# Two attention blocks run twice on one core: quartered loads, a redrawn plan, and a first chunk of x that is turned by TensorE

## The chip, the core and the metric

One core of a Trainium2 chip runs the whole program. The metric is the device time of one execution in microseconds, lower being better. Several executions are made of each kernel and the median is compared; beside them stands one execution that was recorded by the hardware profiler, from which all durations here are taken.

## The reference

x has 2048 rows of 1024 bf16 values. Four blocks follow each other, A, B, A, B, each adding its result to x:

```
x = x + A(layernorm(x), A_wqkv, A_w_phi, A_wo)
x = x + B(layernorm(x), B_wqkv, B_wo)
x = x + A(...)      # the same weights as the first time
x = x + B(...)

A: q,k,v = x @ wqkv, 32 heads of 32 columns
   phi(t) = [softmax(t @ w_phi), softmax(-t @ w_phi)]
   out = phi(q) @ (phi(k)^T v) / (phi(q) . sum phi(k)),  then @ wo
B: ordinary softmax attention over 2048 keys, 32 heads of 32 columns, then @ wo
```

Block A is linear in the rows: its cost is projections. Block B needs 32 x 2048 x 2048 exponentials each time.

## The kernel before, in words

x is kept transposed in SBUF the whole time, in `xT`: 128 partitions, 8 groups of 128 columns of x (`PO`), 2048 rows. The rows are worked in four chunks of 512 (`NC`). Everything else lives in one big SBUF tile, `arena`, and one PSUM tile of eight banks, which the program divides itself.

**A planner sets the order.** The kernel function doesn't issue instructions; it records operations with `op(engine, duration, function, dependencies, buffers, priority)`. `Sched.run` (line 152) then plays a list schedule with those assumed durations: at each moment each engine takes, among the operations that are ready and whose buffers can be had (quotas in `QUOTA`, line 302), the one with the lowest priority number. The sequence in which operations start in that play is the sequence in which instructions are issued to the engines, and `_alloc` (line 77) fixes the buffers' addresses in the same play. So a change of one assumed duration can change the order of all that comes later, on every engine, and the addresses. Loads go through `dma` (line 474), on SyncE's queue ("SP") or ScalarE's queue ("AQ"); the planner assumes 0.55 us for an issue and 2 us plus a time by size for the landing.

**The first layer's start.** `load_x` (line 510) loads x with transposing DMAs on SyncE's queue: eight for the first chunk of 512 rows (one for each of the 8 column groups), eight for the second, eight for the last two together. Four small loads bring `w_phi` into `phi` (line 1215). `fold_phi` (line 599) multiplies the key part of A's weights, Wk, with the block-diagonal `phi`: two loads of 1 MB on ScalarE's queue bring Wk as it lies (line 603), 64 TensorE transposes in eight groups of eight turn it (line 612), each group is copied out of PSUM, in turn by ScalarE (line 620) and VectorE (line 617), 64 matmuls multiply (line 639), and ScalarE and VectorE in turn write the results (lines 646 and 649) into two slabs that hold 512 columns each. The slabs are also stored to DRAM (line 653) for the second time block A runs. `layernorm` (line 526) of a chunk: squares on ScalarE (line 538, in two halves here, n=2), 8 matmuls with a matrix of ones for the mean and 8 for the mean square (through `mmgroup`, line 480), mean and its square on ScalarE (559, 561), variance on VectorE (562), logarithm and exponential on ScalarE (564, 566), then for each quarter a subtraction and a multiplication on VectorE (572, 576). `a_keys` (line 668) then takes, for each 128 rows and 512 columns, 8 matmuls with the Wk slab and 8 with the Wv slab, two exponentials on ScalarE (688), a sum, a reciprocal and a product on VectorE (692, 695, 701). Matmuls of the plain kind all show as line 480, those that run on four column strips as line 484.

**The rest.** `a_queries`, `a_out`, and the projections of block B follow; then `attention` (line 1066) for 32 heads: scores in PSUM (line 1104), one exponential over three banks on ScalarE (line 1113), the product with V and with ones (line 1145), and its copy by VectorE (line 1161). Part of the exponentials is done on VectorE instead (`exp_dve`, lines 1047 to 1061). While ScalarE works through them, TensorE fills in other projections, among them the keys of the next block A. When TensorE has too little to do, the planner puts in matmuls that change nothing (line 1377). The second layer repeats all this, with its own constants.

**Loads of weights.** `slab` (line 582) loads 1024 rows by n columns of a weight as 128 partitions x 8 groups x n, with one DMA: 1 MB at n=512, 256 KB at n=128. It returns the load four times, one for each pair of the 8 groups, so that matmuls can depend on it pair by pair; before, the four are the same DMA. For the second layer, the normalized chunks 0 to 2 of block A come back from DRAM with one load of 1 MB each (line 1262).

Of the kernel before, what the change touches and what calls it, by code (L numbers as in the profile page):

```python
# [3 lines left out]

# [41 lines left out]
SWITCH = 0.1  # L46
AGAIN = 0.2
RING = 0.5
LOOK = 8


class Sched:
# [97 lines left out]
            b.at = None  # L150

    def run(self):
        engines = list(LAT)
        ready = {e: [] for e in engines}
        busy = {e: 0.0 for e in engines}
# [25 lines left out]
        while left:  # L181
# [109 lines left out]
NUMS = 2  # L291
# [7 lines left out]
EVAC = 20.0  # L299
QA = (40.0, 7.0)  # L300
KVG = 0.14
QUOTA = {"pk": 3, "pv": 2, "kv": 1, "ln": 2, "mm": 4, "cmp": 2, "bc": 4, "num": NUMS, "wt": 4, "fil": 2,
         "e": 6, "vp": 6, "e1": 4, "vp1": 4, "E": 6, "q2": 3, "kt": 3, "w2": 6, "w2o": 3, "oT": 27, "T": 4, "den": 2,
         "lnt": 6, "lnw": 2, "lnw1": 1, "eq": 16, "ns": 4, "cw": 6, "hl": 6, "oc": 2, "slab": 7, "slabk": 3, "fin": 4,
         "rs": 8, "pkf": 1, "cden": 2, "part": 8, "w2r": 1,
# [22 lines left out]
def dve_us(n):  # L328
    return n / 960 + 0.15
# [6 lines left out]
def kernel(  # L336
# [137 lines left out]
    def dma(prio, fn, deps=(), bufs=(), q="SP", kb=256, issue=0.55):  # L474
        return op(q, issue, fn, deps, bufs, prio, lat=2.0 + kb / 200.0)
# [32 lines left out]
    xdone = [None] * NC  # L508

    def load_x():  # L510
        for lo, hi, prio, us, kb in ((0, 1, -24.0, 1.3, 128), (1, 2, -9.0, 1.3, 400), (2, NC, -8.0, 2.0, 800)):
            last = []
            for po in range(PO):
                last.append(dma(
                    prio, lambda lo=lo, hi=hi, po=po: nc.sync.dma_start_transpose(
                        out=xT[:, po, lo * C512:hi * C512], in_=A_x[0, lo * C512:hi * C512, po * P:(po + 1) * P]),
                    issue=us, kb=kb))
            for c in range(lo, hi):
                xdone[c] = last
# [61 lines left out]

    def slab(cls, prio, src, n, deps=(), q="SP"):
        b, v = sb(cls, PO, n)
        o = dma(prio, lambda: (nc.sync if q == "SP" else nc.scalar).dma_start(out=v(), in_=src),
                deps, [b], q=q, kb=2 * n)
        return b, v, [o] * 4


    def slab_turned(cls, prio, src, n):
# [9 lines left out]
    def fold_phi(col, wd_v, prio, use_pe):  # L599
        w_t = []  # L600
        if use_pe:
# [4 lines left out]
            for g in range(G):  # L606
                tb, tv = ps("wt", ANY)

                def tr(g=g, tv=tv):
                    o = tv().bitcast(BF16)  # L610
                    for po in range(PO):
                        nc.tensor.transpose(
                            out=o[:, po * P:(po + 1) * P], in_=nv()[:, po, g * P:(g + 1) * P], identity=ident[:])
                t1 = op("PE", 8 * 0.11, tr, [ld[g // 4]], [tb, nb], prio, mode="n")
                wb, wv_ = sb("wT", D)
                if g % 2:
                    t2 = op("DVE", dve_us(1024), lambda tv=tv, wv_=wv_: nc.vector.tensor_copy(
                        out=wv_(), in_=tv().bitcast(BF16)), [t1], [tb, wb], prio)
                else:
                    t2 = op("ACT", act_us(1024), lambda tv=tv, wv_=wv_: nc.scalar.copy(  # L620
                        out=wv_(), in_=tv().bitcast(BF16)), [t1], [tb, wb], prio)
                w_t.append((wb, wv_, t2))
# [609 lines left out]
    for layer in range(2):  # L1232
# [14 lines left out]
            wv_s = [wv_slab(base + fc * 0.5, fc) for fc in range(2)]  # L1247
            chunks = range(NC - 1, NC)
        for c in chunks:
            xnA[c] = layernorm(c, base + 10 * c - 9 if base + c else -16.0, ANY, n=4 if layer else 2)  # L1250
            a_keys(c, base + 10 * c, wk_s, wv_s, kv, ANY)
        state = a_state(kv, base + 32)

# [3 lines left out]
        else:  # L1257
            wq_s = [slab("slab", second - 15 + fc, wdq_v[:, :, fc * C512:(fc + 1) * C512], C512, [store["q"][fc]])
                    for fc in range(2)]
            for c in range(NC - 1):  # L1260
                x_b, x_v = sb("xn", PO, C512)
                xnA[c] = (x_b, x_v, [dma(second - 20 + 20 * c, lambda c=c, x_v=x_v: nc.sync.dma_start(
                    out=x_v(), in_=xd_v[:, c, :, :]), [xnA[c]], [x_b], kb=1024)] * 4)
        wo_s = [slab_turned("slab", second - 6 + fc, A_o[:, :, fc * C512:(fc + 1) * C512], C512) for fc in range(2)]
        bv_s = [slab("slab", second - 4 + 134 * fc, B_w[:, :, 2 * D + fc * C512:2 * D + (fc + 1) * C512], C512)
                for fc in range(2)]
# [146 lines left out]
```

## Time and profile before

| what | value |
|---|---|
| median of 3 executions | 2373.57 us (2373.34 to 2375.6) |
| the profiled execution's own time | 2381.73 us |
| its span, first to last instruction | 2379.9 us |
| mean granted TensorE clock | 0.989 |
| TensorE busy | 2241.8 us (94%) |
| ScalarE busy | 2072.2 us (87%) |
| VectorE busy | 1669.0 us (70%) |

How to read it: the profiled execution is 8.16 us longer than the median, so differences are worked out in its own times and then taken off the median. "Busy" of TensorE contains modelled ends of pipelined matmuls. A row of a view of stretches gives, for each engine, the busy microseconds and in brackets how many instructions started; then the granted clock (PEclk, 1.00 is full), the mean busy share of the 16 DMA engines and what they moved. A row of the view in order of time gives the start, the duration of a run of like instructions, engine, line, operation, output and input, and in square brackets the idle time before it and what ended that. Rows that begin with SPq or ACTq are DMAs as they are issued on that engine's queue.

### The profile page before, as it was taken

What the parts mean: (1) busy time and instruction counts of PE and PEld (TensorE: products, weight loads), DVE (VectorE), ACT (ScalarE), POOL (GpSimd) and SP (SyncE); (2) the same over time, 40 slices, a digit from 0 to 9 for tenths busy, and PEclk for the clock granted to TensorE, in tenths of its full rate; (3) what the DMA queues carried; (4) which work ended last, traced back from release to release, by engine and by line L of the source; (5) the groups of instructions that cost most, each with busy time, mean ns of one, the idle gap of its engine ahead of it and who ended that gap; (6) DMA issues with size and microseconds to landing.
All of it is one profiled execution on the core that took longest, in us unless ns stands there. A gap on an engine that the chain in (4) does not pass through costs nothing.

```text
span 2379.9 us, 67117 instructions
## 1 busy us (share of the span) xinstructions
PE 2241.8 (94%) x29746; PEld 872.4 (37%) x29816; DVE 1669.0 (70%) x2135; ACT 2072.2 (87%) x1850; POOL 25.2 (1%) x70
## 2 busy tenths in 40 slices
PE   7999999999999999999998999999999999899998
PEld 4443343333333333333333434433333333333333
DVE  7987752345678676764764776489888988977763
ACT  5436559999999999999997555899999999999998
POOL 0000000000000000000000000000000000000000
PEclk9999999999999999999999999999999999999999
DMA  9210101122131222213323001110111101111111
GB/s 213 64 37 1 32 21 36 29 52 53 44 92 54 57 59 68 82 55 86 112 73 108 28 3 34 31 27 25 36 27 31 33 25 29 40 50 44 38 30 35
DMA packets 218092, 118.69 MB, mean 50 GB/s; under 512 B 139208, under 2 KB 208840, under 8 KB 217032
## 3 DMA queue, kind: packets, MB, share of 16 engines
q1 hardware_dynamic: 215720, 112.29, 17.6%
q8 instruction: 233, 3.82, 0.7%
q10 hardware_dynamic: 2080, 2.10, 0.3%
q14 instruction: 59, 0.48, 0.1%
HBM read 78.71 MB, written 14.14 MB: 39 GB/s over the span
## 4 chain that ended last, share of the span: by engine, by line
ACT 26%; PE 16%; issue 6%; DVE 5%; DMA 1%; SPq 0%; ACTq 0%; DVEq 0%; another core or an unknown queue 0%
ACT arena L1113 25%; PE psum L480 8%; PE psum L484 2%; PE psum L1145 2%; PE psum L1104 2%; DVE arena L1058 2%; DVE arena L1061 1%; DMA arena<-rd 1%; DVE arena L1047 1%; DVE arena L1050 0%; ACT arena L688 0%; DVE arena L1202 0%; PE psum L857 0%; PE psum L1377 0%; DVE arena L1161 0%
## 5 line engine op out<-in xcount | busy, mean ns | idle before, releaser
L1113 ACT ACTIVATE arena<-psum 128x1536 bf16<-128x1536 f32 x1295 | 1749.4, 1670 | 20.5 <-PE psum L1104 12.9
L1145 PE MATMUL psum<-arena 128*32 128x512 bf16 x4096 | 626.7, 386 | 12.1 <-DVE arena L1161 7.6
L1145 PE MATMUL psum<-arena,ones_bf 128*32 128x512 bf16 x4096 | 626.6, 386 | 1.3 <-issue 1.3
L484 PE MATMUL psum<-arena 128*32 128x512 bf16 (+1 forms) x9792 | 590.0, 356 | 6.5 <-DVE arena L920 3.0
L1104 PE MATMUL psum<-arena 32*128 32x512 bf16 x3884 | 513.9, 384 | 84.0 <-ACT arena L1113 75.0
L480 PE MATMUL psum<-arena 128*128 128x512 bf16 (+1 forms) x1969 | 446.6, 376 | 10.8 <-DVE arena L1182 3.6
L1058 DVE SCALAR_TENSOR_TENSOR arena<-arena 128x1024 f32<-128x1024 f32 x318 | 387.7, 1219 | 6.3 <-PE psum L1145 2.2
L1104 PEld LDWEIGHTS <-arena 32*128 32x128 bf16 x3884 | 173.7, 91 | 572.5 <-issue 561.4
L484 PEld LDWEIGHTS <-arena 128*32 128x32 bf16 x9792 | 221.6, 96 | 231.0 <-issue 120.0
L480 PEld LDWEIGHTS <-arena 128*128 128x128 bf16 x2032 | 190.6, 98 | 245.6 <-issue 45.9
L1145 PEld LDWEIGHTS <-arena 128*32 128x32 bf16 x4096 | 166.8, 95 | 247.1 <-issue 191.1
L1047 DVE TENSOR_SCALAR arena<-psum 128x512 int32<-128x512 f32 x212 | 145.8, 688 | 80.4 <-PE psum L1040 69.6
L920 DVE CAST arena<-psum 128x512 bf16<-128x512 f32 x120 | 82.5, 687 | 155.7 <-PE psum L484 141.7
L1145 PEld LDWEIGHTS <-ones_bf 128*32 128x32 bf16 x4096 | 163.8, 95 | 30.3 <-issue 15.9
L1061 DVE SCALAR_TENSOR_TENSOR arena<-arena 128x1024 bf16<-128x1024 f32 x106 | 129.3, 1220 | 3.5 <-PE psum L1145 0.2
L688 ACT ACTIVATE arena<-psum 128x512 bf16<-128x512 f32 x80 | 43.0, 597 | 87.5 <-PE psum L480 66.6
L1161 DVE COPY arena<-psum 128x512 f32<-128x512 f32 x126 | 86.4, 686 | 44.1 <-PE psum L1145 43.0
L1377 PE MATMUL psum<-xT,zero 128*32 128x512 bf16 x1360 | 111.5, 384 | 0.0
L1202 DVE TENSOR_TENSOR arena<-arena 64x512 bf16<-64x512 f32 x124 | 84.7, 683 | 34.4 <-DMA arena<-rd 21.0
L692 DVE TENSOR_REDUCE arena<-arena 128x32 f32<-128x1024 bf16 x64 | 77.7, 1214 | 32.5 <-ACT arena L688 31.0
L814 ACT ACTIVATE arena<-psum 128x512 bf16<-128x512 f32 x128 | 69.4, 597 | 31.4 <-PE psum L480 30.6
L572 DVE TENSOR_TENSOR arena<-xT,arena 128x1024 f32<-128x1024 bf16 x64 | 77.8, 1219 | 24.4 <-ACT arena L561 23.8
(102 smaller groups left out, 1359.4 us busy)
## 6 DMA issues: line engine op xcount, KB each, us to landing
arena<-rd SPq DMA_DIRECT2D x62, 256.0 KB
arena<-in_B_wqkv_dram SPq DMA_DIRECT2D x48, 256.0 KB
arena<-in_A_wqkv_dram SPq DMA_DIRECT2D x10, 1024.0 KB
arena<-arena SPq DMA_DIRECT2D x256, 32.0 KB
arena<-in_B_wo_dram SPq DMA_DIRECT2D x32, 256.0 KB
arena<-wd_k SPq DMA_DIRECT2D x8, 1024.0 KB
arena<-arena SPq DMA_DIRECT2D x96, 64.0 KB
arena<-in_B_wqkv_dram SPq DMA_DIRECT2D x4, 1024.0 KB
```

Of the source, the lines that this page charges most:

```text
L480: nc.tensor.matmul(out_, lhsT=lhsT, rhs=rhs, start=start, stop=stop, skip_group_check=True)
L484: nc.tensor.matmul(out_[ks, :], lhsT=lhsT[:, ks], rhs=rhs, start=start, stop=stop, tile_position=(0, 32 * k), skip_group_check=True)
L920: return op("DVE", dve_us(512), lambda: nc.vector.tensor_copy(out=dst(), in_=src()), [dep], bufs, prio)
L1047: ys.append(op("DVE", dve_us(512), lambda k=k, s_v=s_v: nc.vector.tensor_scalar(out=y_v()[:, k, :].bitcast(I32), in0=s_v(), scalar1=POW2_B ...
L1058: last = [op("DVE", dve_us(1024), lambda i=i, c=c: nc.vector.scalar_tensor_tensor(out=x_v(), in0=(x_v() if i else m_v()), scalar=c, in1=m_ ...
L1061: eo = op("DVE", dve_us(1024), lambda: nc.vector.scalar_tensor_tensor(out=e_v(), in0=x_v(), scalar=POW2_0, in1=y_v(), op0=ALU.add, op1=ALU ...
L1104: nc.tensor.matmul(out=s_v()[:, x * C512:(x + 1) * C512], lhsT=kT[g][1]()[r, pp, d * P:(d + 1) * P], rhs=q_of[(qc, g)][1]()[r, (pp + j // ...
L1113: ex = op("ACT", act_us(w * C512), lambda s_v=s_v, e_v=e_v, w=w: nc.scalar.activation(out=e_v()[:, 0:w * C512], in_=s_v(), func=ACT.Exp, s ...
L1145: nc.tensor.matmul(out=a_v()[col:col + 32, :], lhsT=v_v()[:, kc % 4, o:o + DH] if what == 0 else ones_bf[:], rhs=ev()[:, x * C512:(x + 1) ...
L1161: cp = op("DVE", dve_us(512), lambda t_v=t_v, a_v=a_v: nc.vector.tensor_copy(out=t_v(), in_=a_v()), [last], [a_b, t_b], prio - 4)
L1202: s = [op("DVE", dve_us(512), lambda a=a, k=k, o_v=o_v, r_v=r_v, T=T: nc.vector.tensor_tensor(out=o_v()[a, :], in0=T[k][1]()[a, :], in1=r_ ...
L1377: nc.tensor.matmul(psum[32 * k:32 * k + 32, 6 * C512:7 * C512], lhsT=zero[:], rhs=xT[:, 0, 0:C512], start=False, stop=False, tile_position ...
```

## The change

Five edits. `slab` splits a load of 512 columns into four of 256 KB, each two of the 8 groups, and returns the four; loads of 128 columns stay whole. The return of the normalized chunks is split in the same way. `load_x` brings the first chunk of x as it lies, as four loads of 128 rows x 1024 columns (256 KB) in turn on SyncE's and ScalarE's queue, turns it with 32 TensorE transposes in four groups of eight, and copies the groups out of PSUM in turn on ScalarE and VectorE; the other chunks keep their transposing DMAs. The norm of chunk 0 works by quarters (n=4). Wk's turned groups are copied by ScalarE, but for the last, which VectorE copies. And the planner's assumed duration of every operation on VectorE and TensorE is multiplied by a drawn number between 0.99 and 1.01, from a generator with the seed `TIE`.

```diff
+TIE = 9
@@ Sched.run
+        draw = random.Random(TIE)
+        for o in self.ops:
+            if TIE and o.eng in ("DVE", "PE"):
+                o.dur *= 1 + draw.uniform(-0.01, 0.01)
@@
-QUOTA = {"pk": 3, "pv": 2, "kv": 1, "ln": 2, "mm": 4, "cmp": 2, "bc": 4, "num": NUMS, "wt": 4, "fil": 2,
+QUOTA = {"xt": 4, "pk": 3, "pv": 2, "kv": 1, "ln": 2, "mm": 4, "cmp": 2, "bc": 4, "num": NUMS, "wt": 4, "fil": 2,
@@ load_x
-        for lo, hi, prio, us, kb in ((0, 1, -24.0, 1.3, 128), (1, 2, -9.0, 1.3, 400), (2, NC, -8.0, 2.0, 800)):
+        n_b, n_v = sb("xnat", TB, D)
+        got = [dma(-24.0, lambda t=t: (nc.sync, nc.scalar)[t % 2].dma_start(
+            out=n_v()[:, t, :], in_=A_x[0, t * P:(t + 1) * P, :]), (), [n_b], q=("SP", "AQ")[t % 2], kb=256) for t in range(TB)]
+        first = []
+        for i in range(PO // 2):
+            t_b, t_v = ps("xt", ANY)
+
+            def tr(i=i, t_v=t_v):
+                o = t_v().bitcast(BF16)
+                for k in range(2):
+                    for t in range(TB):
+                        nc.tensor.transpose(
+                            out=o[:, (4 * k + t) * P:(4 * k + t + 1) * P],
+                            in_=n_v()[:, t, (2 * i + k) * P:(2 * i + k + 1) * P], identity=ident[:])
+            t1 = op("PE", 8 * 0.1, tr, got, [t_b, n_b], -24.0, mode="n")
+
+            def cp(i=i, t_v=t_v):
+                return dict(out=xT[:, 2 * i:2 * i + 2, 0:C512], in_=t_v().bitcast(BF16).rearrange("p (k n) -> p k n", k=2))
+            if i % 2:
+                c = op("DVE", dve_us(1024), lambda cp=cp: nc.vector.tensor_copy(**cp()), [t1], [t_b], -24.0)
+            else:
+                c = op("ACT", act_us(1024), lambda cp=cp: nc.scalar.copy(**cp()), [t1], [t_b], -24.0)
+            first += [c, c]
+        xdone[0] = first
+        for lo, hi, prio, us, kb in ((1, 2, -9.0, 1.3, 400), (2, NC, -8.0, 2.0, 800)):
@@ slab
-        o = dma(prio, lambda: (nc.sync if q == "SP" else nc.scalar).dma_start(out=v(), in_=src),
-                deps, [b], q=q, kb=2 * n)
-        return b, v, [o] * 4
+        if n < C512:
+            o = dma(prio, lambda: (nc.sync if q == "SP" else nc.scalar).dma_start(out=v(), in_=src),
+                    deps, [b], q=q, kb=2 * n)
+            return b, v, [o] * 4
+        return b, v, [dma(prio + 0.001 * i, lambda i=i: (nc.sync if q == "SP" else nc.scalar).dma_start(
+            out=v()[:, 2 * i:2 * i + 2, :], in_=src[:, 2 * i:2 * i + 2, :]),
+            deps, [b], q=q, kb=n / 2) for i in range(4)]
@@ fold_phi
-                if g % 2:
+                if g == 7:
@@ the layers
-            xnA[c] = layernorm(c, base + 10 * c - 9 if base + c else -16.0, ANY, n=4 if layer else 2)
+            xnA[c] = layernorm(c, base + 10 * c - 9 if base + c else -16.0, ANY, n=4 if layer or c == 0 else 2)
@@
-                xnA[c] = (x_b, x_v, [dma(second - 20 + 20 * c, lambda c=c, x_v=x_v: nc.sync.dma_start(
-                    out=x_v(), in_=xd_v[:, c, :, :]), [xnA[c]], [x_b], kb=1024)] * 4)
+                xnA[c] = (x_b, x_v, [dma(second - 20 + 20 * c + 0.001 * i, lambda c=c, x_v=x_v, i=i: nc.sync.dma_start(
+                    out=x_v()[:, 2 * i:2 * i + 2, :], in_=xd_v[:, c, 2 * i:2 * i + 2, :]),
+                    [xnA[c]], [x_b], kb=256) for i in range(4)])
```

1 line of the change is left out of this document (added).

## The prediction, made before the changed kernel had run

> **What bounds the kernel now.** I read the page's slices first, to see which engine is full where; then long stretches, for how full; then the first 36 us in order of time, because four of the five edits meet there; then the clock and the loads.
>
> ```profile
> span 2379.9 us, 67117 instructions
> ...
> PE   7999999999999999999998999999999999899998
> ...
> ACT  5436559999999999999997555899999999999998
> ```
>
> ```profile
> 30.00:120.00 90.00, 87.22 (x935) 43.78 (x944) 83.23 (x96) 40.31 (x64) 6.18 (x19) 1.00 0.52 114
> 120.00:350.00 230.00, 226.24 (x1834) 94.72 (x1862) 170.40 (x229) 118.82 (x203) 4.22 (x13) 1.00 0.07 21
> 360.00:1270.00 910.00, 858.30 (x13072) 316.85 (x13068) 550.60 (x697) 896.87 (x700) 11.51 (x24) 0.99 0.23 65
> ...
> 1520.00:2360.00 840.00, 788.63 (x11633) 293.62 (x11625) 666.66 (x823) 835.54 (x622) 0.00 (x0) 0.99 0.12 33
> ```
>
> The columns are the stretch, its length, and the busy time of TensorE, its weight loads, VectorE, ScalarE and GpSimd. Projections, to about 350 us: TensorE has 87.2 of 90 and 226.2 of 230. Attention: ScalarE has 896.9 of 910 and 835.5 of 840, so it is idle 13.1 + 4.5 = 17.6 us there. The ends of the chain are thus TensorE, then ScalarE, twice. A microsecond by which TensorE reaches its steady work earlier at the start is a microsecond off the end; whatever only loads SyncE's queue or VectorE is hidden, unless it tears a hole into one of these two.
>
> The one large hole is at the start.
>
> ```profile
> 0.00:10.00 10.00, 3.23 (x31) 3.24 (x32) 4.98 (x36) 2.75 (x3) 0.70 (x6) 1.00 0.78 206
> 10.00:20.00 10.00, 6.72 (x55) 5.12 (x54) 2.77 (x4) 5.30 (x5) 0.00 (x0) 0.83 1.06 284
> 20.00:30.00 10.00, 7.39 (x59) 4.52 (x59) 8.77 (x9) 9.03 (x14) 0.00 (x0) 0.85 0.99 160
> ```
>
> ```profile
> 27.00:31.00 4.00, 3.90 (x16) 1.69 (x15) 3.97 (x4) 3.87 (x3) 0.00 (x0) 0.57 0.64 136
> ```
>
> ```profile
> 0.74 10.39 SPq L515 DMA_TRANSPOSE xT<-in_A_x_dram  x8
> 0.76 7.03 ACTq L603 DMA_DIRECT2D arena<-in_A_wqkv_dram  x2
> ...
> 6.76 3.50 PE L612 MATMUL psum<-ident,arena 128*128 128x128 bf16 x32 [6.76 <-DMA arena<-in_A_wqkv_dram]
> 7.84 1.01 ACT L620 COPY arena<-psum 128x1024 bf16<-128x1024 bf16 x1 [5.82 <-PE psum L612]
> 8.69 0.69 DVE L617 COPY arena<-psum 128x1024 bf16<-128x1024 bf16 x1 [3.01 <-PE psum L612]
> ...
> 13.49 3.54 PE L612 MATMUL psum<-ident,arena 128*128 128x128 bf16 x32 [3.23 <-DMA arena<-in_A_wqkv_dram]
> ...
> 16.87 1.89 PE L480 MATMUL psum<-xT,onesD 128*128 128x512 bf16 x7
> ...
> 17.18 3.71 ACT L538 ACTIVATE arena<-xT 128x2048 bf16<-128x2048 bf16 x2
> ...
> 20.79 0.59 ACT L559 ACTIVATE arena<-psum 128x512 f32<-128x512 f32 x1
> ...
> 21.73 2.07 ACT L646 CAST arena<-psum 128x512 bf16<-128x512 f32 x4
> ...
> 23.75 0.72 ACT L564 ACTIVATE arena<-arena,eps 128x512 f32<-128x512 f32 x1
> ...
> 24.50 0.63 ACT L566 ACTIVATE arena<-arena 128x512 f32<-128x512 f32 x1
> ...
> 25.36 2.35 DVE L576 TENSOR_TENSOR arena<-arena 128x1024 bf16<-128x1024 f32 x2
> ...
> 27.20 2.34 PE L480 MATMUL psum<-arena 128*128 128x512 bf16 x5
> ...
> 31.28 1.22 DVE L576 TENSOR_TENSOR arena<-arena 128x1024 bf16<-128x1024 f32 x1
> ...
> 35.76 13.54 PE L480 MATMUL psum<-arena 128*128 128x512 bf16 x60
> ```
>
> TensorE is busy 3.23 + 6.72 + 7.39 us of the first 30: idle 12.7. Between 27 and 31 it ran at 0.57 of its clock, which wastes 0.43 x 4 = 1.7. Lost together: 14.4 us. Why: Wk's first half serves from 6.76, its second only from 13.49, since the second load was issued at the end of the 7.03 us that the two took. x needs eight transposing DMAs, 1.3 us of issue each, 10.39 in all, so its norm starts at 17.18, the first normalized quarter ends at 25.36 + 1.18 = 26.5, the last at 31.28 + 1.22 = 32.5, and the first key matmul waits until 27.20.
>
> **The change, part by part.**
>
> *x as it lies.* Removed: eight transposing DMAs. Added: four plain loads, 32 transposes on TensorE, four copies. No row shows a 256 KB load at an empty start; the rows nearest to it are the rates:
>
> ```profile
> 2.00:3.00 1.00, 0.00 (x0) 0.00 (x0) 0.85 (x5) 0.01 (x1) 0.00 (x0) 1.00 0.75 265
> ...
> 5.00:6.00 1.00, 0.00 (x0) 0.00 (x0) 0.63 (x2) 0.00 (x0) 0.00 (x0) 1.00 1.15 344
> ```
>
> 1.05 MB at 265 to 344 GB/s from 2.0 us on is there at 5.0 to 6.0; I take 5.6. The 32 transposes cost 3.5 us, as the row of 6.76 has it for as many, and end at 9.1, the last copy (VectorE, 0.69) at 9.8, seven microseconds ahead of 16.87. This is 3.5 us more work for the engine that bounds the stage.
>
> [...]
>
> *The norm by quarters.* Four squares instead of two:
>
> ```profile
> L538 ACT ACTIVATE arena<-xT x32: 1056/1908/1957, 17.2 to 1496.7; 128x2048 bf16<-128x2048 bf16 x20, 128x1024 bf16<-128x1024 bf16 x12
> ```
>
> The quarter is the shortest, 1.06 us, so 4.2 instead of 3.7, but the first starts after the first copy. ScalarE begins when the first eight transposes are through, at 5.6 + 0.9 = 6.5: two copies of x (2.0, by the row of 7.84) and the squares (4.2) end at 12.7. From the end of the squares to the first normalized quarter it was 26.5 - 20.9 = 5.6, to the last 11.6: now 18.3 and 24.3 instead of 26.5 and 32.5, eight earlier.
>
> *Wk's copies.* Seven by ScalarE (7.1 us) instead of four (4.0). Nothing hides them but ScalarE's own idleness, which is 10 - 2.75 and 10 - 5.30 in the first two rows of ten. Before a key matmul can start, ScalarE must have done: copies of x 2.0, squares 4.2, mean and its square 1.2 (twice the row of 20.79), logarithm and exponential 1.35 (23.75 and 24.50), four Wk copies 4.05, four results of the fold 2.1 (21.73), together 14.9, so at 21.4 if it never stops. That is later than the 18.3 of the norm, and 5.8 earlier than 27.20. ScalarE sets the start of the keys, no longer x.
>
> *What TensorE gains.* The same work as up to 35.76, plus 3.5. It loses 5.6 before x, 3.5 for x, and about 1.0 between the last transpose of x and the first of Wk: 10.1 against 14.4, a gain of **4.3**. Bounds: no pause at all gives 5.3; a pause of 3 until ScalarE's copies come, and the half clock once more (1.7), leaves 0.6. What is late next is VectorE, full from then on:
>
> ```profile
> 80.00:120.00 40.00, 37.82 (x457) 19.78 (x460) 37.89 (x46) 14.78 (x27) 2.93 (x9) 1.00 0.29 83
> ```
>
> TensorE misses 2.2 here, where VectorE has 37.9 of 40 and is behind. VectorE's subtractions start eight earlier and its work has hardly grown (two copies of x more, three of Wk fewer), so I count **2.0** of this as won; bounds 0 and 2.2.
>
> *Loads in quarters.*
>
> ```profile
> arena<-in_A_wqkv_dram SPq DMA_DIRECT2D x10, 1024.0 KB
> ...
> arena<-in_B_wo_dram SPq DMA_DIRECT2D x2, 1024.0 KB
> ```
>
> ```profile
> L584 SPq DMA_DIRECT2D arena<-in_A_wqkv_dram x10: 378/469/588, 13.8 to 1187.9; - x10
> ```
>
> These are the first and the last of six such rows of loads into the arena (10, 8, 4, 3, 2 and 2). 29 loads become 116: 87 more issues of 0.47 us, 41 us of a queue with 2380. What stands behind such a load on the queue (the returns of the denominators, the keys, the next weights) comes 1.4 us later each time. In the other direction, the first matmul of a slab can start on the first quarter. In the view of waits the only long one for a weight load is that for Wk at the start:
> ```profile
> PEld L612 <- DMA arena<-in_A_wqkv_dram: 10.2, 2, 6.8
> ```
>
> The 10.2 us are two waits, and they are in the sum above. So I count **0** for the quarters; bounds: one place on the path gains or loses 1.4.
>
> [...]
>
> *The redrawn plan.* One per cent of noise changes which ready operation is taken first, all the way down. It adds no work. It moves where TensorE has a gap long enough to lose its clock:
>
> ```profile
> 1080.00:1120.00 40.00, 36.06 (x594) 12.47 (x594) 21.70 (x28) 36.92 (x29) 0.00 (x0) 0.96 0.29 79
> ...
> 1160.00:1200.00 40.00, 36.57 (x484) 12.83 (x480) 27.49 (x35) 36.13 (x32) 1.65 (x4) 0.91 0.48 155
> ...
> 1960.00:2000.00 40.00, 38.14 (x498) 12.39 (x494) 35.38 (x44) 39.21 (x31) 0.00 (x0) 0.96 0.10 25
> ```
>
> In the second of them the clock is 0.91 and ScalarE lacks 3.9 of 40. The first and the last are those of the eight 40 us stretches of attention with a clock under 1.00; ScalarE lacks 3.1 and 0.8 in them. Nearly all of its 17.6 us of idle time lies in the eight, 2.2 each. A draw can have five such spells or eleven; I take eight again, **0**, with 6.6 either way.
>
> **Sum:** 4.3 + 2.0 + 0 + 0 = 6.3 off the profiled execution's 2381.7. Its span is 2379.9; execution and span differ by 1.8, and it stands 8.2 above the median of the runs, where I take off the same: 2373.6 - 6.3 = **2367.3**.
>
> **The rivals.**
>
> *A better draw.* Three spells fewer: 2367.3 - 6.6 = 2360.7. For it: spells are few and each is set by a single late VectorE copy or the like. Against it: nothing in the edit aims at them.
>
> *ScalarE eats the gain.* Its 14.9 us are not packed; TensorE pauses 3 us and more for Wk's copies and falls back to half clock: 0.6 is left, 2373.0. For it: 9.03 of 10 busy between 20 and 30 already. Against it: half the copies wait on nothing but ScalarE.
>
> *The plain load brings nothing.* The DMA engines, not the turning, set when x comes: their mean busy share is 1.06 between 10 and 20. x then comes with the 16.87 of before and 3.5 are added: 2377.1. Against it: the eight issues alone take 10.39. [...]
>
> *Slower: the draw tears holes into attention.* VectorE's copies of finished sums come late, TensorE pauses, loses its clock, and ScalarE's idle time rises from 17.6 by 13 (six spells at 2.2): 2367.3 + 13.2 = 2380.5. It decides from five added spells (11) on, or two if the start gives only 0.6. For it: VectorE is 667 of 840 busy in the second attention, so there is little slack. Against it: six more on top of eight is much for noise of one per cent.
>
> **How the numbers follow.** Forecast 0.48, a better draw 0.25, ScalarE eats it 0.10, the load brings nothing 0.04, slower 0.13. A measurement can tell about 0.2% from no change, 4.75 us: faster is below 2368.8, slower above 2378.3. The forecast's own range, 2362 to 2373, puts 0.36 below and 0.12 within; with the better draw faster is 0.61, same 0.12 + 0.10 + 0.04 = 0.26, slower 0.13. The range goes to six spells fewer, about 2353, and to the slower case's 2380.
>
> **What would show it.** Right: x's transposes on TensorE start by 6 us, the norm's first square near 7.5, the first key matmul near 22, and attention, which begins after the stretch up to 350 quoted above, six earlier. Wrong: a pause of TensorE over 3 us between 9 and 22, or no shift left at 350. The pieces: a wait of TensorE for a weight load, or none. The draw: the number of 40 us stretches of attention with a clock under 1.00, and the idle time of ScalarE in them; if that moves by more than 6.6, the start is not what decides.

## The result, and the profile after

The changed kernel took 2379.93 us (median of 10 runs, 2377.07 to 2382.91), the kernel before 2374.8 beside it (10 runs, 2369.76 to 2378.05): ratio 1.0020, 95% interval 1.0012 to 1.0028. It is slower by about 5 us. The forecast was 2367.3, faster; the time lies at the upper end of the range, where the prediction had put the case "the draw tears holes into attention". The profiled execution took 2380.89, its span is:

```profile
span 2379.1 us, 67094 instructions
...
PE   8999999999998999889998999999999999899998
...
ACT  6336559999998999999998555799999999999998
```

The span is nearly that of before, 2379.9, only because the execution of before that was profiled stood 8.2 above its median. So a stage of the one is to be compared with a stage of the other with a few microseconds of doubt, and the experiments below carry more than this pair.

**The start.** The changed kernel in order of time (start, length, what, count, and in brackets the idle time before it and what ended that):

```profile
0.74 0.87 SPq L518 DMA_DIRECT2D arena<-in_A_x_dram  x2
0.76 0.88 ACTq L518 DMA_DIRECT2D arena<-in_A_x_dram  x2
...
1.67 1.09 ACTq L637 DMA_DIRECT2D arena<-in_A_wqkv_dram  x2
...
4.30 0.47 PE L528 MATMUL psum<-ident,arena 128*128 128x128 bf16 x2 [4.30 <-DMA arena<-in_A_x_dram]
...
5.95 3.46 PE L528 MATMUL psum<-ident,arena 128*128 128x128 bf16 x30 [1.18 <-DMA arena<-in_A_x_dram]
...
7.93 1.06 ACT L568 ACTIVATE arena<-xT 128x1024 bf16<-128x1024 bf16 x1
...
9.79 2.95 ACT L568 ACTIVATE arena<-xT 128x1024 bf16<-128x1024 bf16 x3
...
18.24 3.73 ACT L654 COPY arena<-psum 128x1024 bf16<-128x1024 bf16 x4
18.37 2.36 DVE L606 TENSOR_TENSOR arena<-arena 128x1024 bf16<-128x1024 f32 x2 [1.35 <-ACT arena L596]
...
19.29 0.61 PE L646 MATMUL psum<-ident,arena 128*128 128x128 bf16 x8 [1.13 <-ACT arena L654]
...
20.42 1.03 PE L486 MATMUL psum<-arena 128*128 128x512 bf16 x3
```

The loads of x are issued in 0.9 us where the transposing ones took 10.4, and both halves of Wk by 2.8 where the second had gone out only at the end of the 7.03 us. The first key matmul runs at 20.42 instead of 27.20. All that came as forecast. But TensorE won next to nothing by it. Each row is a stretch, in the columns that the prediction names; ScalarE is the fourth of them:

```profile
0.00:10.00 10.00, 4.53 (x34) 3.69 (x35) 5.45 (x37) 4.36 (x5) 0.70 (x6) 1.00 0.84 277
10.00:20.00 10.00, 8.20 (x78) 5.42 (x78) 4.80 (x6) 9.57 (x12) 0.00 (x0) 1.00 1.22 275
20.00:30.00 10.00, 7.96 (x63) 4.54 (x64) 9.23 (x11) 7.27 (x9) 0.00 (x0) 1.00 0.82 122
80.00:120.00 40.00, 39.01 (x454) 19.71 (x455) 38.23 (x45) 13.83 (x25) 2.91 (x9) 1.00 0.35 94
360.00:1270.00 910.00, 848.65 (x12896) 311.16 (x12889) 548.75 (x694) 889.15 (x695) 11.84 (x24) 0.99 0.23 64
1520.00:2360.00 840.00, 789.28 (x11740) 295.82 (x11742) 668.68 (x825) 838.53 (x625) 0.00 (x0) 1.00 0.13 33
```

In the first 30 us TensorE's columns give 9.3 us of idle time, against 12.7 before: 3.4 less. The 32 transposes of x are 0.47 + 3.46 = 3.9 us of new work. ScalarE is at 9.57 of 10 between 10 and 20: it sets the pace there, and TensorE waits for its copies of Wk (1.13 us at 19.29).

**The attention.** The two long stretches have ScalarE idle for 20.9 + 1.5 = 22.3 us, 17.6 before. The first and the last exponential of attention, kernel before and then after (the times at the end of the count are the first and the last start):

```profile
L1113 ACT ACTIVATE arena<-psum x1295: 1371/1670/2013, 353.3 to 2366.3; 128x1536 bf16<-128x1536 f32 x185
```

```profile
L1147 ACT ACTIVATE arena<-psum x1295: 1430/1671/2019, 352.4 to 2365.3; 128x1536 bf16<-128x1536 f32 x185
```

Attention begins 0.9 us earlier, where 6.3 were forecast. The order alone also moves this time: among the runs below, draw9, with the old start, begins it at 349.5, and after_draw2, with the new one, at 358.1. Only plan_start and plan_all, which keep the old order, show what the start is worth apart from the order.

### The profile page after: what moved, and what is told of

The parts are those of the page before. It is cut to its first block, busy times and chain, and to the rows that moved or that the text cites. A ratio compares the mean times of both kernels' runs of the same rounds, so it can differ in the third digit from the quotient of the medians.

```text
span 2379.1 us, 67094 instructions
## 1 busy us (share of the span) xinstructions
PE 2233.5 (94%) x29677; PEld 868.3 (36%) x29744; DVE 1668.4 (70%) x2134; ACT 2076.8 (87%) x1857; POOL 25.5 (1%) x70
## 4 chain that ended last, share of the span: by engine, by line
ACT 38%; PE 38%; DVE 9%; issue 9%; DMA 5%; SPq 1%; ACTq 0%; DVEq 0%; another core or an unknown queue 0%
ACT arena L1147 37%; PE psum L486 19%; PE psum L490 6%; PE psum L1179 5%; PE psum L1138 4%; DMA arena<-rd 3%; DVE arena L1092 3%; DVE arena L1081 1%; DVE arena L1236 1%; PE psum L891 1%; DVE arena L1095 1%; ACT arena L722 1%; PE psum L755 1%; DVE arena L1084 1%; DVE arena L954 1%
## 5 line engine op out<-in xcount | busy, mean ns | idle before, releaser
L1412 PE MATMUL psum<-xT,zero 128*32 128x512 bf16 x1296 | 104.6, 380 | 0.0
L602 DVE TENSOR_TENSOR arena<-xT,arena 128x1024 f32<-128x1024 bf16 x64 | 77.9, 1218 | 25.9 <-ACT arena L591 25.2
```

The source lines that it names most:

```text
L1412: nc.tensor.matmul(psum[32 * k:32 * k + 32, 6 * C512:7 * C512], lhsT=zero[:], rhs=xT[:, 0, 0:C512], start=False, stop=False, tile_position ...
```

## The experiments

The prediction summed five edits and counted the noise in the planner's durations at nothing. My theory after the result: **the noise costs what the other edits win, and more**; it orders VectorE's and SyncE's work so that the denominators of a finished pair come back too late. Rivals: the edits themselves cost (the start, or the 87 further loads on SyncE's queue, which stand before urgent transfers); or the noise is harmless and the new plan is slower by itself.

All ratios are to the kernel before, run on the same chip. 0.2% is 4.75 us.

### The noise alone, and everything but the noise

`draw9` is the kernel before with the five added lines of the planner's loop and `TIE = 9`. `nodraw` is the changed kernel with

```
-TIE = 9
+TIE = 0
```

> The kernel before with the drawn durations alone (seed 9), whole loads and the old start. Theory R (the redrawn order of attention, in which VectorE stands longer waiting for the denominators' return, costs the 5 us): slower than before by 3 to 8 us, with VectorE's wait for that return well above the 21 us of before. Rival P (the quartered loads delay what stands behind them on SyncE's queue): within 2 us of before. Rival S (the new start costs it): within 2 us of before.

> The changed kernel with the noise switched off (seed 0), all other edits kept; the plan is still another than before, since loads and start are planned differently. Theory R: any order is a draw, so this lands between 6 us faster and 8 us slower than before, and its time follows ScalarE's idle time in attention. Rival P: slower by 4 to 6 us as the changed kernel is. Rival S: slower by 4 to 6 us too, and the lag is there already when attention begins (about 353 us before).

Measured: draw9 **1.0029** (1.0016 to 1.0043), nodraw **0.9963** (0.9952 to 0.9974; a second measurement of the same kernel gave 0.9970, 0.9960 to 0.9980). So the edits without the noise are 0.37% faster, nearly 9 us, and the noise costs 0.29% (7 us) on the old plan and 1.0020/0.9963, 0.57% (13 us), on the new one. The rows of the attention's exponentials on the pages of before, draw9, changed and nodraw (busy time and mean ns of one, then the engine's idle time just ahead of them):

```profile
L1113 ACT ACTIVATE arena<-psum 128x1536 bf16<-128x1536 f32 x1295 | 1749.4, 1670 | 20.5 <-PE psum L1104 12.9
```

```profile
L1119 ACT ACTIVATE arena<-psum 128x1536 bf16<-128x1536 f32 x1295 | 1750.9, 1660 | 33.6 <-PE psum L1110 27.0
```

```profile
L1147 ACT ACTIVATE arena<-psum 128x1536 bf16<-128x1536 f32 x1295 | 1751.3, 1666 | 24.0 <-PE psum L1138 10.2
```

```profile
L1147 ACT ACTIVATE arena<-psum 128x1536 bf16<-128x1536 f32 x1295 | 1751.3, 1699 | 13.0 <-PE psum L1138 9.1
```

The busy time is about 1750 in all four; what moves is the idle time. From nodraw to the changed kernel it grows by 11.0, and the span by 2379.1 - 2368.6 = 10.5: with this seed the noise costs about as much as ScalarE's idle time in attention grows. From before to draw9 it grows by 13.1 and the span only by 5.8: attention begins 3.8 us earlier in draw9, and the profile of before stands 8.2 above its median, that of draw9 2.7. VectorE waits for the denominators' return for 38.2 us in draw9 and 21.0 before, as theory R had it. Where the changed kernel's idle time lies shows in five 40 us stretches (480, 720, 1000, 1040 and 1080 on) in which the changed kernel's clock is under 1.00, first the changed kernel, then nodraw, each as the sum of the five:

```profile
720.00:760.00 40.00, 34.95 (x455) 11.24 (x451) 25.77 (x32) 33.72 (x26) 0.00 (x0) 0.91 0.26 64
...
sum 200.00, PE 178.76 PEld 66.03 DVE 117.84 ACT 182.41 POOL 4.15; mean PE 35.75 PEld 13.21 DVE 23.57 ACT 36.48 POOL 0.83
```

```profile
720.00:760.00 40.00, 37.96 (x517) 12.55 (x513) 30.44 (x38) 39.99 (x31) 0.00 (x0) 1.00 0.25 71
...
sum 200.00, PE 190.14 PEld 71.09 DVE 134.96 ACT 199.28 POOL 4.20; mean PE 38.03 PEld 14.22 DVE 26.99 ACT 39.86 POOL 0.84
```

ScalarE lacks 17.6 of 200 with the noise and 0.7 without. The worst of the five, 720 to 760, in order of time in the changed kernel:

```profile
729.13 0.46 SPq L1231 DMA_DIRECT2D rd<-arena  x1
...
730.77 0.59 SPq L1233 DMA_DIRECT2D arena<-rd  x1
...
731.41 1.50 SPq L618 DMA_DIRECT2D arena<-wd_k  x3
...
735.38 2.79 ACT L1147 ACTIVATE arena<-psum 128x1536 bf16<-128x1536 f32 x2 [1.47 <-PE psum L490]
...
738.30 0.68 DVE L1236 TENSOR_TENSOR arena<-arena 64x512 bf16<-64x512 f32 x1 [4.19 <-DMA arena<-rd]
738.91 0.68 DVE L962 TENSOR_SCALAR arena<-psum 128x512 bf16<-128x512 f32 x1
...
739.64 0.62 PE L490 MATMUL psum<-xT,onesD 128*32 128x512 bf16 x4 [3.45 <-DVE arena L962]
...
741.44 1.45 ACT L1147 ACTIVATE arena<-psum 128x1536 bf16<-128x1536 f32 x1 [3.28 <-PE psum L1179]
```

This is how a hole forms. The denominators' return (L1233) is issued at 730.77 among quarters of a bulk load. VectorE has reached the multiply that needs it and stands 4.19 us until 738.30; the next operation in its line, L962, copies a sum out of the accumulator that TensorE needs next, so TensorE stands 3.45 us, and ScalarE 3.28 ahead of 741.44. (The 1.47 ahead of 735.38 are not part of it: they end while VectorE still stands.) In the trace two more of the holes in these stretches have the same order: VectorE waits 2.75 us for a return until 512.72, TensorE 1.61, ScalarE 1.86, and 5.24, 2.89 and 2.74 from 1066.45 on. The one at 1007, where ScalarE stands 2.03, has not: TensorE's pause of 2.81 ahead of it waits for nothing that the profile shows. What comes out of the pause runs on a slow clock, 0.57 in the mean of these 8 us (the column behind GpSimd's):

```profile
738.00:746.00 8.00, 6.36 (x53) 1.59 (x56) 6.69 (x7) 3.48 (x4) 0.00 (x0) 0.57 0.15 38
```

### The loads alone, the start alone, and both, all in the old order

`plan_pieces` keeps the planner's operations, order and addresses of before and only issues four transfers where one stood:

```
+        def load():
+            for i in range(4 if n == C512 else 1):
+                s = slice(2 * i, 2 * i + 2) if n == C512 else slice(0, PO)
+                (nc.sync if q == "SP" else nc.scalar).dma_start(out=v()[:, s, :], in_=src[:, s, :])
+        o = dma(prio, load, deps, [b], q=q, kb=2 * n)
```

(the reload of xn likewise). `plan_start` keeps the same order and does the start alone: the operation of the first transposing load issues four plain ones, that of the fifth the 32 transposes and four copies, the squares go by quarters, and seven copies of Wk go to ScalarE. `plan_all` does both.

> The kernel before in its own planned order and addresses, with no noise; only the DMAs differ: each load of 1 MB is issued as four of 256 KB at the place of the one. Theory R: within 2 us of before. Rival P: slower by 3 to 6 us, the denominators' return landing later than the 5.0 us median of before.

> The kernel before in its planned order and addresses, with whole loads; only the start is changed (x's first chunk as it lies, squares by quarters, Wk's copies on ScalarE). If the start is what made the version with all edits in the old plan 0.28% faster: 4 to 7 us faster than before, and attention begins 2 us or more earlier than at 353. If the quartered loads and the start share it (the quarters alone gave 0.13%): 3 to 4 us faster. If the start gives only what the trace shows at the beginning of attention: 2 us faster.

> All edits but the noise, in the planned order and addresses of before: quartered loads, x's first chunk as it lies and turned by TensorE (held in the part of xT that is still empty), the squares by quarters, Wk's copies on ScalarE. Theory R: 0 to 3 us faster than before, since the start gains about 1 us and nothing is reordered. Rival P: slower by 3 to 6 us. Rival S: slower by 2 us or more, with attention starting later than 353 us. The forecast's own step (the start is worth 6.3 us) would give 6 us faster.

Measured: plan_pieces **0.9987** (0.9975 to 0.9999), plan_start **1.0004** (0.9995 to 1.0013), plan_all **0.9972** (0.9962 to 0.9982). Neither part costs anything that the intervals show, so that rival falls, also by its sign: the median return of the denominators lands 5.1 us after its issue with quarters and 5.0 before (by the trace's record of landings). The rival of a new plan that is slower by itself falls by nodraw: its plan is made anew too, and it has 0.9963. The start alone is worth nothing in the time: attention begins 1.5 us earlier in its trace (351.8), and its exponentials stand idle 18.2. The quarters gain about 3 us, hardly clear of nothing. The two together gain 0.28%, where their sum is 0.09%; the difference is hardly more than the intervals allow, and what they might do for each other stays open.

### The wait for the denominators taken away

`after_nowait` and `nodraw_nowait` issue the same operations in the same order, but the reciprocal and the multiply read constants, so that VectorE has nothing to wait for there. They leave out block B's division by its denominators:

```
-... nc.vector.reciprocal(out=c_v(), in_=c_v()) ...
+... nc.vector.reciprocal(out=inv[:], in_=eps[:].to_broadcast([P, 16])) ...
-... in_=c_v()), [rc], [c_b], kb=8)
+... in_=inv[:]), [rc], [c_b], kb=8)
-... in1=r_v()[a, :], op=ALU.mult),
+... in1=eps[a, :].to_broadcast([64, C512]), op=ALU.mult),
```

> The changed kernel (noise seed 9) in which VectorE no longer waits for the denominators: its reciprocals and the multiplications of block B read a constant in place of what the DMAs bring, the DMAs are still issued, so block B's output isn't divided by its denominators. Theory W (VectorE standing at those two lines, 43.5 + 26.9 us in the changed kernel, tears the holes into attention that the noise makes): 8 to 13 us faster than the changed kernel, close to the same edit of the version without noise. Rival O (the order of the other operations tears them): at most 4 us faster than the changed kernel, and the distance to the version without noise stays at 7 us or more.

> The same edit in the version without noise (block B's output isn't divided by its denominators here either). Theory W: it gains less than the changed kernel does, 0 to 4 us against its own 2368.9, since its holes are few already. Rival O: it gains about as much as the changed kernel does by the edit.

Measured: after_nowait **0.9969** (0.9958 to 0.9981), nodraw_nowait **0.9949** (0.9931 to 0.9966). Without the waits the changed kernel gains 0.51%, 12 us, as theory W had it, and the noise-free one 0.14%, 3 us, which the intervals don't tell from nothing. The distance between the two shrinks from 0.57% to 0.20%, by which about two thirds of what the noise costs would come through these waits; with some 0.2% of uncertainty in the 0.20%, it may be all. The traces give less: the spans of the two pairs differ by 10.5 us with the waits and 2367.8 - 2361.5 = 6.3 without, and in the five stretches above ScalarE still lacks 11.4 of 200 without them (17.6 with them, 0.7 in nodraw). So a part of the cost comes through the waits, and how large it is stays open. What is left is seen at the same place, where the wait is gone and the hole is still there (after_nowait, in order of time):

```profile
732.50 4.13 ACT L1148 ACTIVATE arena<-psum 128x1536 bf16<-128x1536 f32 x3 [1.47 <-PE psum L491]
...
738.13 0.95 PE L491 MATMUL psum<-arena 128*32 128x512 bf16 x8 [3.19 <-DMA arena<-in_B_wqkv_dram]
...
739.73 1.45 ACT L1148 ACTIVATE arena<-psum 128x1536 bf16<-128x1536 f32 x1 [3.10 <-PE psum L1139]
```

Now TensorE stands 3.19 us for a small load of block B's weights that was issued at 730.80, behind the last three quarters of the bulk load (from 729.25 on). That the sum of the waits does not order the times speaks against them as the whole cause too. For the multiplies of the pages of before, the changed kernel and nodraw:

```profile
L1202 DVE TENSOR_TENSOR arena<-arena 64x512 bf16<-64x512 f32 x124 | 84.7, 683 | 34.4 <-DMA arena<-rd 21.0
```

```profile
L1236 DVE TENSOR_TENSOR arena<-arena 64x512 bf16<-64x512 f32 x124 | 84.7, 683 | 49.2 <-DMA arena<-rd 43.5
```

```profile
L1236 DVE TENSOR_TENSOR arena<-arena 64x512 bf16<-64x512 f32 x124 | 84.8, 684 | 40.4 <-DMA arena<-rd 34.4
```

nodraw waits longer for the returns than before (34.4 against 21.0) and is faster; after_draw5, below, waits 35.1, as long as nodraw, and is 0.82% slower. The prices differ within one trace too: the waits of 3.77 us at 426 and 3.49 at 597 in the changed kernel bring no pause of ScalarE over 0.8 us, those of 4.19 and 5.24 do.

### Bulk loads later

The hole at 730 to 740 names the bulk load as a culprit. `after_late` and `nodraw_late` issue each quarter 2.5 us later in the plan's order, all else as it was:

```
-    for o in sch.run():
+    for o in sorted(sch.run(), key=lambda o: o.start + o.late):
```

with `late` = 2.5 for the quarters of the slabs and 0 else.

> The changed kernel with its plan, order and addresses on every engine but one thing: each quarter of a 1 MB weight load is issued 2.5 us later in the plan's time, behind the small urgent DMAs (denominators' return, 256 KB weights for TensorE) that the plan puts within that time. Theory C (bulk loads issued just ahead of urgent ones make them land up to 3 us later, and that tears some of the holes, the one at 735 to 747 us above all): 4 to 8 us faster than the changed kernel. Rival O (the order of the compute engines): within 2 us of the changed kernel.

> The same delay of bulk loads in the version without noise. Theory C: 0 to 3 us faster than that version, which has few such holes, so 0.995 to 0.9965 of before. Rival O: the same as that version. If holes sit wherever timing puts them: slower by up to 5 us.

Measured: after_late **1.0007** (0.9996 to 1.0019), nodraw_late **0.9979** (0.9970 to 0.9989). The first gains 0.13%, 3 us, less than I expected of the theory; the second loses 0.16%. In the stretch from 720 to 760 ScalarE lacks 3.7 of 40 in place of 6.3: the return, issued at 733.32 ahead of all four quarters, is there for the multiply at 738.92, 5.6 us later in place of 7.5. Elsewhere holes came and went: spells at a low clock are new at 457, 706, 826 and 1280, those at 1036 and 1067 are gone, and the exponentials stand idle 24.3 us in all, 24.0 in the changed kernel. That bulk loads issued with urgent transfers make them late is true at that place and explains little of the sum.

### Other draws

`after_draw2` and `after_draw5` are the changed kernel with `TIE = 2` and `TIE = 5`, `draw2` is the kernel before with noise and `TIE = 2`, and `after_tenth` has a tenth of the noise:

```
-                o.dur *= 1 + draw.uniform(-0.01, 0.01)
+                o.dur *= 1 + draw.uniform(-0.001, 0.001)
```

> The changed kernel with seed 2 for the noise. If any noise harms a plan whose constants were chosen without it: 5 us or more slower than the version without noise, 0.998 of before or above. If a draw is a coin toss around the version without noise: 0.992 to 1.002 of before, the time following ScalarE's idle time in attention.

> The changed kernel with seed 5. The same two cases as for seed 2; if both seeds are slower than the version without noise, three of three are, with seed 9.

> The kernel before with noise of 1%, seed 2, and nothing else. If any draw costs (four of four so far, by 0.29 to 0.82%), 1.002 to 1.005. If draws fall to both sides with the four by chance on one, 0.997 to 1.003, with a value under 1.000 as likely as not.

> The changed kernel with noise of 0.1% in place of 1% on the assumed durations, seed 9 as before. If the wrong durations themselves mislead the list scheduler, a tenth of the error should cost about a tenth of the 0.57% that separates the kernel without noise (0.9963 of the kernel before) from the changed kernel (1.0020): 0.9965 to 0.9975. If it is enough that ties between nearly equal starts fall another way, one draw is as good as another whatever its size: anywhere between 0.998 and 1.0045, where the draws of 1% lay.

Measured: after_draw2 **1.0000** (0.9988 to 1.0013), after_draw5 **1.0045** (1.0029 to 1.0060), draw2 **0.9999** (0.9989 to 1.0010), after_tenth **0.9996** (0.9982 to 1.0011). Against the same plan without noise (1 or 0.9963) the six draws cost 0.29% and nothing on the old plan, and 0.57%, 0.37%, 0.82% and, with a tenth of the noise, 0.33% on the new one. draw2 refutes that any draw costs; that none of six gained is little to go on, and the seeds are no fair sample, since with another, 1, the planner did not come to an end in time and there was no kernel to run. Nor does the loss lie in one place: by the spans after_draw2 is 8.8 us longer than nodraw, and 7.2 of them are there when attention begins (358.1 against 350.9); of after_draw5's 18.7 some 13 lie in the two attentions and 5 between them. A tenth of the noise costs 0.33% (0.26% against the second measurement of nodraw, which ran beside it), where a tenth of 0.57% is 0.06%. With some 0.18% of uncertainty in that difference it only just leaves the proportionate share out: that any other order of nearly equal choices costs, rather than the size of the error, is likely and not settled.

### The return on another queue

`after_pool` has the plan of the changed kernel and issues the store and the return of the denominators from GpSimd's queue:

```
-                aw = dma(prio, lambda c_v=c_v, at_d=at_d: nc.sync.dma_start(
+                aw = dma(prio, lambda c_v=c_v, at_d=at_d: nc.gpsimd.dma_start(
...
-                bk = dma(prio, lambda r_v=r_v, at_d=at_d: nc.sync.dma_start(
+                bk = dma(prio, lambda r_v=r_v, at_d=at_d: nc.gpsimd.dma_start(
```

and `nodraw_gps` has the same edit without noise. (The run labelled nodraw_pool was meant to be that, but executed nodraw as it was: SyncE issues both in its trace. It is the second measurement of nodraw above, and says nothing on its expectation.)

> The changed kernel with the same plan, the store and the return of the denominators issued by GpSimd on its own queue in place of SyncE's. If VectorE waits for the return because it stands behind the quarters of the bulk loads on SyncE's queue, it now lands in about 4 us in place of up to 7.5, the 43.5 us of waits in attention fall by half and the ratio goes from 1.0020 to 0.998 or below. If the planned order itself is what is late, the waits stay at 35 to 50 us and the ratio at 1.000 to 1.004, or above, since what GpSimd's queue costs for a transfer is not shown by any run so far.

> The changed kernel without noise (0.9963 of the kernel before), with the store and the return of the denominators issued by GpSimd on its own queue. Reading constants in their place took it to 0.9949, so that is about what a return that is never late can give: 0.995 if SyncE's queue delays it, 0.996 if the queue is no part of it, above 0.998 if GpSimd's queue itself is slower.

> The changed kernel without noise, with the store and the return of the denominators issued by GpSimd on its own queue: the run labelled nodraw_pool executed the noise-free kernel as it was (SyncE still issues both in its trace), so this is still to be seen. The same edit took the changed kernel with its noise from 1.0020 to 1.0091 of the kernel before. If GpSimd's queue itself is slower (an issue of 0.56 and 0.71 us there against 0.35 and 0.59 on SyncE), the same loss of 0.5 to 0.7% falls here: 1.001 to 1.004 against 0.9963 and 0.9970 without it. If the loss hangs on the drawn order, where more returns are just in time, little of it falls here: 0.996 to 0.999.

Measured: after_pool **1.0091** (1.0071 to 1.0111; 4 runs), nodraw_gps **1.0026** (1.0012 to 1.0040). Both lose 0.6 to 0.7%. GpSimd takes longer over the same issue (nodraw, then nodraw_gps: least, median and most ns):

```profile
L1231 SPq DMA_DIRECT2D rd<-arena x62: 320/344/532, 389.9 to 2334.6; - x62
```

```profile
L1231 POOL DMA_DIRECT2D rd<-arena x62: 557/557/962, 391.3 to 2341.6; - x62
```

and the multiplies of nodraw_gps and of after_pool wait longer:

```profile
L1236 DVE TENSOR_TENSOR arena<-arena 64x512 bf16<-64x512 f32 x124 | 84.8, 684 | 56.9 <-DMA arena<-rd 49.5
```

```profile
L1236 DVE TENSOR_TENSOR arena<-arena 64x512 bf16<-64x512 f32 x124 | 84.7, 683 | 68.4 <-DMA arena<-rd 64.8
```

That is 15.1 and 21.3 us of waits more than with SyncE, for a loss of 0.6% of 2375, 14 us, and 0.7%, 17 us; the two fit, though something else on GpSimd's queue isn't excluded. Taking the returns off SyncE's queue did not make them earlier: in after_pool they landed 4.7 to 8.0 us after their issue, 5.1 in the median, where about 4 was expected. The place of the hole shows it best (after_pool, in order of time):

```profile
731.36 1.95 SPq L618 DMA_DIRECT2D arena<-wd_k  x4
...
731.59 0.71 POOL L1233 DMA_DIRECT2D arena<-rd  x1 [2.18 <-PE psum L1138]
...
739.64 0.68 DVE L1236 TENSOR_TENSOR arena<-arena 64x512 bf16<-64x512 f32 x1 [4.33 <-DMA arena<-rd]
```

The return is now alone on its queue, the four quarters are issued on the other at the same time, and the multiply starts 8.05 us after the return's issue (738.30 - 730.77 = 7.53 in the changed kernel). So it isn't the place in SyncE's queue that makes it late there. That quarters under way at the same time do is likely, by this and by the same place in after_late, and not shown by itself. Most returns aren't late at all: the planner assumes 5.0 us for their landing (2 + 600/200, `kb=600`), and the median in the traces is 4.9 to 5.1 on SyncE's queue. What a late one or a slower queue meets is a planned order without room for it. The loss is about the same with and without noise. So the drawn order does not have less room for a slower return than the noise-free one; both have hardly any. From the end of the reciprocal to the landing of the return the median of 62 was 7.5 us in nodraw and 8.1 in nodraw_gps.

## Why the prediction was wrong, step by step

**The redrawn plan, the step that failed.** "It adds no work ... I take eight again, 0, with 6.6 either way." It added no work and cost 13 us on the new plan, twice the bound. The slower rival had the mechanism and even the price (ScalarE's idle time up by 13; 11.0 measured between nodraw and the changed kernel), and it was given 0.13 because six more spells seemed many. Its 2380.5 lies so near the 2379.93 by luck in part: it stands on the 2367.3 of the sum, which came near for another reason (below). The count of spells was the wrong measure: attention has five 40 us stretches under full clock in the changed kernel, eight before, while ScalarE's idle time rose from 17.6 to 22.3 us; in the worst of the five it lacks 6.3 of 40, not 2.2. (In the eight of before it lacks 15.7 of the 17.6, so 2.0 each.) Nor did the length of a gap alone say where TensorE loses its clock: in the changed kernel its pause of 2.81 us that ends at 1006.80 is followed by full clock (1.00 up to 1012), one of 0.95 us that ends at 1035.88 by 0.50 between 1036 and 1039. What the prediction did not look at was that VectorE stands for returns of the denominators, which land 7.5 us after the reciprocal in the median of nodraw, 7.6 in that of before, and for which the plan leaves no room; the waits row of before, 21.0 us for the returns, was on the page and was not read. Why the order without noise beats each drawn one that was run, but for draw2, stays open. The sign named for the draw, 6.6 us in ScalarE's idle time, was not reached by the pair of profiles (4.7), one of which stands 8.2 above its median; against nodraw, which differs in the noise alone, it was (11.0).

**What TensorE gains, 4.3, was mis-sized.** Its parts came as worked out: x's transposes from 4.30 and mainly from 5.95 (by 6), the first square at 7.93 (7.5), the last ended at 12.74 (12.7), the first key matmul at 20.42 (22). What was missing are TensorE's pauses after it has begun: in the rows above it is idle 9.3 us up to 30 where the sum had 5.6 + 1.0. They are spread over waits for ScalarE's copies and for VectorE's quarters, none over 1.2 us before the one of 1.79 that ScalarE ends at 30.59. A further spell at a low clock, 0.57 between 32 and 36, falls into this row, of which the sum had hoped to be free:

```profile
30.00:40.00 10.00, 8.87 (x50) 4.74 (x51) 6.72 (x8) 6.09 (x13) 0.32 (x1) 0.83 1.18 216
```

By the sum's own terms the changed kernel loses 9.3, 3.9 for x's transposes and about 1.7 in that row (0.17 of the clock for 10 us), 14.9 in all against 14.4 before: nothing is won, a little less than the lower bound of 0.6. The rival "ScalarE eats the gain" had that and the low clock, if not the many short pauses. (The 14.4 leaves out that the clock of before was 0.57 between 13 and 17 as well; the 32 transposes there took 3.54 us against 3.50 at full clock, so nothing is seen to be lost by it.) VectorE's lead, 2.0 by the sum, gave 1.2 (TensorE misses 1.0 between 80 and 120 instead of 2.2). Attention begins 0.9 us earlier in the changed kernel, 1.5 in plan_start (351.8), 1.9 in plan_all (351.4) and 2.4 in nodraw (350.9): in the order of before the start brings 1.5 to 1.9 us up to there, not 6.3, and plan_start's time shows none of it (1.0004).

**Loads in quarters, counted at 0:** about 3 us gained in the old order, with an interval that ends at 0.01% (nearly nothing). The bound of one place and 1.4 us was too narrow.

**The sum without the noise was nearly right, for another reason.** 6.3 was forecast, 8.8 is what nodraw has (0.9963), but only about 2.4 of it at the start of attention. The rest lies in attention, where the exponentials stand idle 13.0 instead of 20.5. Which of the edits brings that, the quarters or the order that the planner finds with them, is not settled: plan_pieces has 0.13% of it, plan_all 0.28%.

**The plain load brings nothing:** it does; x's norm starts at 7.93, nine microseconds earlier than 17.18. Two plain loads took 0.87 us of SyncE's queue, eight transposing ones 10.39.

**The best version** that was run and leaves nothing out is nodraw, the change without its noise: 0.9963 of the kernel before, 0.57% under the changed kernel. plan_all, at 0.9972, is not clearly behind it.

## What to carry to other kernels

Where a planner orders the work, its assumed durations are part of the kernel: price a redrawn order as a cost of its own, by running the edits in the old order and the new order without the edits, and don't count it as nothing because it adds no work. An earlier start was worth little here, where the next engine in line had no room (ScalarE at 9.57 of 10 us, the first key matmul 6.8 us earlier, attention 0.9): sum that engine's work over the stretch, and count the pauses after the first arrival, not only the one before it. In a loop that is bound by one engine, read the idle time ahead of that engine's main instruction first; here, over all 18 profiles, the span grows by 1.0 us with each microsecond of it and strays from that line by -4 to +6 us, and it followed neither the sum of another engine's waits nor the number of spells at a low clock.

## What was not expected of the hardware

- The profiles' idle time ahead of the 1295 exponentials was 13.0 in nodraw (span 2368.6), 20.5 before (2379.9), 24.0 in the changed kernel (2379.1), 33.6 in draw9 (2385.7) and 39.4 in after_pool (2394.3), with the busy time between 1749.4 and 1752.2 in all five. after_draw5 strays most: 25.2 at a span of 2387.3, with part of its loss outside attention.
- A return of the denominators that was issued among the quarters of a 1 MB load landed 7.5 us after its issue (730.77 to 738.30), where the median of the 62 is 4.9. Issued at the same place on GpSimd's own queue, beside the quarters on SyncE's, it took 8.0.
- Four times as many loads of a quarter of the size cost nothing that the runs show: 87 more issues of 0.45 to 0.48 us (medians in the changed kernel), and plan_pieces was at 0.9987 (0.9975 to 0.9999).
- Moving 62 stores of 8 KB and 62 returns of 256 KB from SyncE's queue to GpSimd's, which issued no other DMA, cost 0.6 to 0.7%.
